# Later weight parts, earlier last stores and a moved row transpose in an RWKV and mixture-of-depths kernel

## The chip, the cores and the metric

The kernel runs on one core of one Trainium2 chip. The metric is the device time of one execution in microseconds (us); lower is better. A core has engines that each work through their own list of instructions in order: PE (matrix products and transposes), DVE (vector), ACT (scalar), POOL and SP, which here only issues transfers between the chip's memory (DRAM) and the on-chip buffers. Engines wait for each other through semaphores. Transfers are carried out by 16 DMA engines, which work beside all others.

## The reference

Two steps follow each other. The first is a linear attention over 768 time steps for 4 batches and 8 heads of 48 columns, with a state that decays:

```python
for t in range(S):
    kt, vt, rt = (k[:, :, t], v[:, :, t], r[:, :, t])
    cur = np.einsum('bhd,bhe->bhde', u[None] * kt, vt)
    y[:, :, t] = np.einsum('bhd,bhde->bhe', rt, state + cur)
    state = w[None, :, :, None] * state + np.einsum('bhd,bhe->bhde', kt, vt)
```

The second takes y, as rows of 384 columns, and lets the 128 rows with the highest score of each batch (of 768) pass through a two-layer network with 1024 hidden columns:

```python
scores = np.einsum('bsd,d->bs', x, w_gate)
out = x.copy()
for b in range(B):
    top_idx = np.argpartition(-scores[b], capacity)[:capacity]
    xe = x[b, top_idx]
    h = np.maximum(xe @ w1, 0.0)
    ye = h @ w2
    g = 1.0 / (1.0 + np.exp(-scores[b, top_idx]))
    out[b, top_idx] = x[b, top_idx] + g[:, None] * ye
```

All numbers are in 32-bit floating point.

## The kernel before

The time steps are cut into blocks of 128. There are 6 blocks in a batch and 24 in all (`NC` = 6, `NU` = 24). The main loop has one iteration per block. The order of all instructions on every engine is the order in which the program writes them down; no scheduler moves them.

**One iteration.** In iteration i PE finishes y of block i-1: first the products with the state (`from_state`, "y L287" from z and rh), then the score products of block i ("rp L259"), then the products with the values (`from_values`, "y L287" from vin and at). It then transposes k and r of block i+1 (`turn`, "L240", to the banks pt and st or ea), and makes the sums for the next state. These last exist in two forms: `state_product` (L269, 32 small matmuls in the profile, before the value products), used when `late` is true, and `state_products` (L282, 16 wider ones, after the turns) otherwise. `late` is true when work of the network is waiting in `queue` as the iteration begins. POOL writes half of the at-tile of the block (`diagonals`, L234), DVE writes the masked scores over it (`masked`, L302), and ACT copies y out (`leave_y`, the x-tile). At the end of an iteration POOL prepares k and r of block i+2 (L209, L213, L215). If `queue` is empty, PE ends the iteration with three products that nobody reads (`unread`, L264), in a bank that the next scores will use; they wait until DVE has read the bank's last contents.

**Choosing rows.** Scores are compared while the blocks come in. When a batch is complete, at iteration e+3 with e its last block (8, 14 and 20 for the first three batches), its rows are ranked (`rank`, `one_hot`), PE picks the indices (`pick`, L405), and POOL gathers the chosen rows from DRAM (`fetch`, an indirect transfer to xr, L417). For the first batch the pick stands at the end of iteration 8; for the others in the middle of theirs, behind up to two pieces of the network of the batch before. The gather reads what the stores of y have written, so it waits for the stores of its own batch. The program tells the dependency tracker that stores of other batches touch other rows. One iteration after the gather, at the place "chosen" at the end of the iteration, PE transposes the rows (`chosen`, L434, to bank pt), ACT copies them (xt), and `enqueue` puts 16 pieces into `queue`: eight times `hidden` (128 hidden columns, L467) and eight times `expert` (one product with 128 rows of the second matrix, L477). From then on every iteration takes its share of pieces, three in each of four iterations and two in each of the next two.

**The transfers.** All loads and stores of the loop are issued by SP, in the order in which they are written. At the head of iteration i these are k and r of block i+4 (L85, L86), v of block i+3 (two transfers, L92), some parts of the network's weights (L199 for the first matrix, L201 for the second), and the store of y of block i-2 (`store_y`, L335). SP runs through this list on its own; it only waits for buffers and for the x-tile that it stores. Inputs have six buffers, x has four.

**The weights.** Both matrices stay on the chip. They arrive in 20 parts: twelve of 128 rows and 256 columns of the first (128 KB each), ordered by groups of 256 columns and within a group by three blocks of rows, and eight of 128 rows of the second (192 KB each). `WEIGHTS` says how many parts iteration i issues. `hidden` with index f needs the three parts of its group (parts 0 to 2 for f = 0 and 1, 3 to 5 for f = 2 and 3, 6 to 8, 9 to 11), and `expert` with index f needs part 12+f. The tracker follows each part on its own: a product waits for the parts that it reads.

Of the kernel before, what the change touches and what calls it, by code (L numbers as in the profile page):

```python
# [17 lines left out]
def kernel(  # L18
# [16 lines left out]
    NC = S // T  # L35
# [42 lines left out]
    def load_kr(n):  # L78
        b, c = divmod(n, NC)
        rows = slice(c * T, (c + 1) * T)  # L80
        if n == 0:
            KIN[n] = kws[NKW - 1][:, :, :D]
        else:
            KIN[n] = work.tile([128, H, D], F32, name="kin", bufs=NIN)
        nc.sync.dma_start(out=KIN[n], in_=k[b, :, rows, :].rearrange("h t d -> t h d"))  # L85
        nc.sync.dma_start(out=rpads[n % NIN][:, :, :D], in_=r[b, :, rows, :].rearrange("h t d -> t h d"))  # L86

    def load_v(n):
        b, c = divmod(n, NC)
        for j in range(2):  # L90
            rows = slice(c * T + j * C, c * T + (j + 1) * C)
            nc.sync.dma_start(out=vins[n % NV][half(j), :, j, :], in_=v[b, :, rows, :].rearrange("h t d -> t h d"))  # L92
# [95 lines left out]
    for hp in range(NP):  # L188
        nc.scalar.activation(tr[:, hp, :C], up[:, hp, :C], AF.Copy, scale=winv[:, 0, hp : hp + 1])

    WEIGHTS = {i: 1 for i in range(3, 9)} | {9: 3, 10: 3, 11: 3, 12: 3, 13: 2}
    parts = [(q, kd) for q in range(4) for kd in range(KD)] + list(range(FB))

    def weights(n):
        for _ in range(n):
            j = parts.pop(0)
            if isinstance(j, tuple):
                f = slice(j[0] * F // 4, (j[0] + 1) * F // 4)
                nc.sync.dma_start(out=w1[:, j[1], f], in_=moe_w1[j[1] * 128 : (j[1] + 1) * 128, f])  # L199
            else:  # L200
                nc.sync.dma_start(out=w2[:, j, :], in_=moe_w2[j * 128 : (j + 1) * 128, :])  # L201
# [9 lines left out]
    def bonus(n):  # L211
        rk = work.tile([128, H, D], F32, name="rk")
        nc.gpsimd.tensor_mul(rk, rpads[n % NIN][:, :, :D], KIN[n])  # L213
        RKU[n] = work.tile([128, H, D], F32, name="rku")
        nc.gpsimd.tensor_mul(RKU[n], rk, ub)  # L215
# [75 lines left out]
    def from_state(n, hp, i, q):  # L291
        c = q ^ i
        z = Z1[n] if c else Z0.get(n)
        if z is not None:
            y_product(n, c, hp, i, RH[n][head(i), hp, half(c)], z[head(i), hp, :])
# [26 lines left out]
    def side(n, i):  # L322
        return YP[n][i][:, : NP * D].rearrange("t (p d) -> t p d", p=NP)
# [9 lines left out]
    def store_y(n):  # L333
        b, c = divmod(n, NC)
        st = nc.sync.dma_start(out=out[b, c * T : (c + 1) * T, :], in_=X[n])  # L335
        for (bb, _), others in moves.items():
            if bb != b:
                for o in others:
                    tc.declare_no_dep(st.ins, o.ins, reason="rows of another batch")
        stores.setdefault(b, []).append(st)  # L340
# [198 lines left out]
    def at(m, place, f, *a):  # L539
        fill.setdefault((m, place), []).append((f, a))  # L540

    def run(m, place):
        for f, a in fill.get((m, place), []):
            f(*a)
# [4 lines left out]
    for b in range(B - 1):  # L549
        e = b * NC + NC - 1  # L550
        at(e + 3, "start", rank, b)
        for z in range(NST):
            at(e + 3, "start", one_hot, b, z)
            at(e + 3, "pick" if b else "chosen", pick, b, z, "pt")
            at(e + 3, "fetch", fetch, b, z)
            at(e + 4, "chosen", chosen, b, z, "pt")
            at(e + 5, "middle", gate_sum, b, z)
            at(e + 6, "gate", gate, b, z)
            at(e + 4, "chosen", enqueue, b, z)

    def share(i):
        n = sum(f is not leave for f, _ in queue)
# [15 lines left out]
    def first():  # L578
        RP[0] = psum.tile([128, 2, 512], F32, name="rp")
        for hp in range(NP):  # L580
            for j in range(2):
                for c in range(2):
                    score_product(0, hp, j, c)
        turned(1, turn(rpads[1], "ea"))
        ST[0] = psum.tile([128, 512], F32, name="st")
        state_products(0)
        Z1[0] = work.tile([128, NP, D], F32, name="z1")
        nc.vector.tensor_copy(Z1[0], sums(0, 0))
        diagonals(0)
        masked(0)  # L590
        G[0] = work.tile([128, NP, D], F32, name="g")
        nc.vector.tensor_add(G[0], sums(0, 1), Z1[0])
        turned_k(1, turn(kws[1], "pt"))
        bonus_sum(1)
        diagonals(1)
        nc.vector.tensor_mul(wc, up[:, :, C], up[:, :, C])  # L596
        nc.vector.tensor_scalar(tri, jp, 0.0, None, op0=OP.is_lt)
        nc.scalar.copy(wg, spread(1, "eb"))
        scaled(2)
        bonus(2)  # L600

    for i in range(NU + 1):
        if i + 4 < NU:
            load_kr(i + 4)
        if i + 3 < NU:
            load_v(i + 3)
        weights(WEIGHTS.get(i, 0))
        if i > 1:
            store_y(i - 2)
        late = bool(queue)  # L610
        if not i:
            first()
            continue
        if i:
            if i < NU:
                t = psum.tile([128, 2, 512], F32, name="y")
                YP[i - 1] = [t[:, 0, :], t[:, 1, :]]
            else:
                YP[i - 1] = [psum.tile([128, 512], F32, name=name) for name in ("pt", "st")]
            for hp in range(NP):  # L620
                for j in range(2):
                    for q in (1, 0):
                        from_state(i - 1, hp, j, q)
            for j in range(1 if i < NU else 2):
                nc.scalar.copy(tiny[:, 1 : 1 + NP], side(i - 1, j)[C : C + 1, :, 0])  # L625
        if i < NU:
            if i not in RP:
                RP[i] = psum.tile([128, 2, 512], F32, name="rp")
            for hp in range(NP):
                for j in range(2):  # L630
                    for c in range(2):
                        score_product(i, hp, j, c)
            if late:
                for hp in range(NP):
                    for c in range(2):
                        for j in range(2):
                            state_product(i, hp, j, c)
        else:
            against_earlier(i - 2)
            score_row(i - 2, "y")  # L640
            against_own(i - 2)
            pieces(1)
        if i:
            for hp in range(NP):
                for c in range(2):
                    for j in range(2):
                        from_values(i - 1, hp, j, c)
        if i and i < NU:
            diagonal(i)
            if i > 3:  # L650
                diagonals(i)
            decays(i - 1)
        if i and i < NU:
            leave_y(i - 1)
            run(i, "gate")
        if i < NU:
            masked(i)
        run(i, "start")
        if late and i < NU:
            states(i)  # L660
        if i + 1 < NU:
            if i:
                turned_k(i + 1, turn(kws[(i + 1) % NKW], "pt"))
            turned(i + 1, turn(rpads[(i + 1) % NIN], "st" if late else "ea"))
        run(i, "turned")
        old = len(ready)
        leaving()
        if i < NU and not late:
            if i:
                ST[i] = psum.tile([128, 512], F32, name="st")  # L670
            state_products(i)
            states(i)
        m = share(i)
        if i < NU and m and (i, "pick") in fill:
            pieces(min(m, 2))
            m -= min(m, 2)
        run(i, "pick")
        if i + 1 < NU:
            bonus_sum(i + 1)
            if i < 3:  # L680
                diagonals(i + 1)
        if i and i < NU:
            gate_score(i - 1)
        run(i, "middle")
        if i < NU:
            pieces(m)
        if 2 <= i < NU:
            against_earlier(i - 2)
            score_row(i - 2, None if late or i != NC + 2 else "ea")
            against_own(i - 2)  # L690
        run(i, "last")
        if i + 1 < NU and not queue:
            RP[i + 1] = psum.tile([128, 2, 512], F32, name="rp")
            unread(RP[i + 1][:, 0, 384:], 3)
        run(i, "chosen")
        if i + 2 < NU:
            scaled(i + 2)
            bonus(i + 2)
        if i == 2:
            clear_v(5)  # L700
        if i == 4:
            numbers()
        send(old)
        run(i, "fetch")

    b, n = B - 1, NU - 1
# [65 lines left out]
```

## Time and profile before

| | us |
|---|---|
| median of three runs | 173.16 |
| the three runs | 173.14, 173.16, 176.85 |
| the profiled execution | 172.11 |
| span of its profile | 170.3 |

| engine | busy us | share of the span |
|---|---|---|
| PE (matmul) | 149.1 | 88% |
| PEld (weight load) | 127.1 | 75% |
| DVE | 110.4 | 65% |
| POOL | 103.9 | 61% |
| ACT | 97.6 | 57% |

The span covers the instructions; the execution's own time is 1.8 us longer. Transfers on SP's queue take 61.7% of the span of the 16 DMA engines, in 81612 packets, most of them under 512 bytes. The mean granted clock of PE is 0.97 of full speed.

In the slices of the profile page each digit is the busy share of a 40th of the span in tenths, and PEclk is the granted clock in tenths of full speed:

```profile
PE   5899999999996189996979967999998998997990
POOL 7999998997660792866562696986558331022022
PEclk9999999999999755999999999999999999999999
DMA  3999799866886997678898996898721112112000
```

A slice is 4.26 us. The profile's chain of waits follows the work that ended last back to what released it. "Issue" in it is time in which an engine waited for nothing that the profile shows. Timelines list instructions in order of time, merged where the same one repeats; the queue of SP lists the issue of each transfer, not its landing.

### The profile page before, as it was taken

The numbers are of one execution on the slowest core, as the hardware profiler recorded it, in microseconds if no ns is written. First come the engines' busy times: TensorE is split into PE (matmuls) and PEld (weight loads), VectorE is DVE, ScalarE is ACT, GpSimd is POOL, SyncE is SP. The second block draws the span as 40 slices with busy tenths as digits, with TensorE's granted clock in tenths as the row PEclk, the third lists the DMA queues.
The fourth block names the chain that finished last, engine by engine and source line by source line (L and its number), as shares of the span: only waits on it lengthen the run. The fifth ranks groups of instructions, "written<-read, shape, count | busy, mean of one in ns | idle before, by whom it ended". The sixth has DMA issues, their size and how long they took to land.

```text
span 170.3 us, 8282 instructions
## 1 busy us (share of the span) xinstructions
PE 149.1 (88%) x3475; PEld 127.1 (75%) x3475; DVE 110.4 (65%) x315; ACT 97.6 (57%) x346; POOL 103.9 (61%) x138
## 2 busy tenths in 40 slices
PE   5899999999996189996979967999998998997990
PEld 3677888988884179996848766998787797756990
DVE  5679988888980354768378479666975796733000
ACT  6656888886757026475637754875676867401200
POOL 7999998997660792866562696986558331022022
PEclk9999999999999755999999999999999999999999
DMA  3999799866886997678898996898721112112000
GB/s 67 179 187 168 143 175 188 198 144 119 191 199 154 183 214 188 144 178 230 183 233 209 206 198 125 182 220 169 157 98 50 50 52 94 48 18 80 0 20 26
DMA packets 82197, 24.13 MB, mean 142 GB/s; under 512 B 76126, under 2 KB 81792, under 8 KB 82160
## 3 DMA queue, kind: packets, MB, share of 16 engines
q1 hardware_dynamic: 81612, 22.03, 61.7%
q0 software_dynamic: 544, 1.57, 3.0%
q8 instruction: 27, 0.44, 1.1%
q14 instruction: 10, 0.08, 0.2%
q10 hardware_dynamic: 4, 0.00, 0.0%
HBM read 18.09 MB, written 5.51 MB: 139 GB/s over the span
## 4 chain that ended last, share of the span: by engine, by line
PE 64%; DMA 12%; issue 9%; DVE 5%; POOL 4%; ACT 3%; POOLq 1%; SPq 0%; ACTq 0%; DVEq 0%
PE y L287 13%; DMA xr<-out_dram,idx 7%; PE ea L467 7%; PE rp L259 6%; PE eb L467 6%; PE pt L240 5%; DMA w<-in_moe_w_dram 5%; PE eb L477 5%; PE st L282 3%; PE rp L269 3%; PE rp L264 3%; PE ea L240 3%; PE st L240 3%; PE ea L477 2%; ACT at L226 1%
## 5 line engine op out<-in xcount | busy, mean ns | idle before, releaser
L302 DVE COPY_PREDICATED at<-mask,rp 128x512 f32<-128x512 uint32 x24 | 17.8, 741 | 29.1 <-ACT at L226 10.1
L234 POOL TENSOR_TENSOR at<-dia,du 128x256 f32<-128x256 f32 x20 | 15.4, 769 | 23.3 <-DVE du L219 11.1
L226 ACT ACTIVATE at<-dia,du 128x64 f32<-128x64 f32 x96 | 25.5, 336 | 1.8 <-DVE du L219 1.8
L209 POOL TENSOR_TENSOR kw<-kin,wk 128x384 f32<-128x384 f32 x23 | 24.8, 1076 | 1.6 <-DMA kin<-in_k_dram 0.8
L215 POOL TENSOR_TENSOR rku<-rk,ub 128x384 f32<-128x384 f32 x24 | 24.5, 1020 | 1.9
L213 POOL TENSOR_TENSOR rk<-rpad,kin 128x384 f32<-128x384 f32 x23 | 23.4, 1016 | 1.5 <-DMA rpad<-in_r_dram 1.5
L318 ACT ACTIVATE z<-g,wc 128x48 f32<-128x48 f32 x80 | 19.9, 319 | 0.4 <-DVE wc L596 0.4
L259 PE MATMUL rp<-rh,kh 48*64 48x64 f32 x768 | 18.4, 229 | 1.0 <-DVE at L302 0.4
L417 POOL DMA_INDIRECT xr<-out_dram,idx x4 | 4.1, 1032 | 21.9 <-DVE part L485 10.1
L287 PE MATMUL y<-vin,at 64*64 64x48 f32 x736 | 16.8, 223 | 0.4 <-issue 0.4
L240 PE MATMUL pt<-ident,kw 128*128 128x128 f32 x96 | 16.6, 298 | 0.5 <-POOL rpad L139 0.4
L287 PEld LDWEIGHTS y<-z,rh 48*64 48x64 f32 x672 | 13.3, 138 | 4.8 <-issue 2.6
L259 PEld LDWEIGHTS rp<-rh,kh 48*64 48x64 f32 x768 | 15.4, 142 | 1.9 <-issue 1.0
L287 PE MATMUL y<-z,rh 48*64 48x48 f32 x672 | 16.3, 227 | 0.3 <-ACT x L331 0.3
L330 ACT COPY x<-y 64x192 f32<-64x192 f32 x46 | 14.4, 314 | 2.5 <-PE y L287 1.1
L344 DVE SCALAR_TENSOR_TENSOR scr<-x,wg 128x384 f32<-128x384 f32 x24 | 15.3, 637 | 0.7 <-ACT x L330 0.4
L287 PEld LDWEIGHTS y<-vin,at 64*64 64x64 f32 x736 | 14.3, 138 | 0.6 <-issue 0.6
L477 PE MATMUL ea<-w,ht 128*128 128x384 f32 x32 | 12.1, 497 | 2.4 <-DMA w<-in_moe_w_dram 2.4
L250 ACT COPY kh<-pt 128x512 f32<-128x512 f32 x23 | 13.6, 590 | 0.8 <-PE pt L240 0.8
L467 PE MATMUL eb<-xt,w 128*128 128x128 f32 x96 | 12.5, 278 | 1.4 <-issue 1.3
L625 ACT COPY tiny<-y 1x4 f32<-1x4 f32 x23 | 3.6, 157 | 17.2 <-PE y L287 17.2
L219 DVE TENSOR_REDUCE du<-rku 128x8 f32<-128x384 f32 x24 | 13.0, 543 | 0.0
(159 smaller groups left out, 306.6 us busy)
## 6 DMA issues: line engine op xcount, KB each, us to landing
rpad<-in_r_dram SPq DMA_DIRECT2D x24, 192.0 KB, 5.0
vin<-in_v_dram SPq DMA_DIRECT2D x48, 96.0 KB, 4.0
out_dram<-x SPq DMA_DIRECT2D x24, 192.0 KB, 3.5
kin<-in_k_dram SPq DMA_DIRECT2D x23, 192.0 KB, 4.3
w<-in_moe_w_dram SPq DMA_DIRECT2D x12, 128.0 KB, 3.4
w<-in_moe_w_dram SPq DMA_DIRECT2D x8, 192.0 KB, 4.1
kw<-in_k_dram SPq DMA_DIRECT2D x1, 192.0 KB
xr<-out_dram,idx POOLq DMA_INDIRECT x4, 3.7
```

What stands on the lines that cost most here:

```text
L209: (nc.gpsimd if n else nc.vector).tensor_mul(kws[n % NKW][:, :, :D], KIN[n], wk)
L213: nc.gpsimd.tensor_mul(rk, rpads[n % NIN][:, :, :D], KIN[n])
L215: nc.gpsimd.tensor_mul(RKU[n], rk, ub)
L226: nc.scalar.activation(AT[n][:, j, :], dia, AF.Copy, scale=du[:, j : j + 1])
L234: eng.tensor_mul(AT[n][:, h:, :], dia[:, None, :].to_broadcast([128, H - h, C]), du[:, h:, None].to_broadcast([128, H - h, C]))
L240: nc.tensor.transpose(t[:, hp, :], x[:, 2 * hp : 2 * hp + 2, :], ident)
L259: nc.tensor.matmul(out=RP[n][s, i, hp * C : (hp + 1) * C], lhsT=KH[n][head(i), hp, s], rhs=RH[n][head(i), hp, s], start=True, stop=True, s ...
L287: nc.tensor.matmul(out=YP[n][i][half(c ^ i), hp * D : (hp + 1) * D], lhsT=lhsT, rhs=rhs, start=(c, i) not in started, stop=True, skip_grou ...
L302: nc.vector.copy_predicated(at, causal, RP[n][:, :, : NP * C].rearrange("s i (p t) -> s i p t", p=NP))
L318: nc.scalar.activation(Z0[n + 1][:, hp, :], G[n][:, hp, :], AF.Copy, scale=wc[:, hp : hp + 1])
L467: nc.tensor.matmul(out=PE[b, z][:, f % 4, :], lhsT=w1[:, d, f * 128 : (f + 1) * 128], rhs=XT[b, z][d], start=(d == 0), stop=(d == KD - 1))
L477: nc.tensor.matmul(out=pe[:, : cols.stop - cols.start], lhsT=HT[b, z][:, f, :], rhs=w2[:, f, cols], start=(f == 0), stop=(f == FB - 1))
```

## The change

Three things are changed. The parts of the weights are issued in iterations 7 to 14 rather than 3 to 13. The stores of the last two blocks of a batch, which fall into iterations e+1 and e+2, are written ahead of the loads of their iteration instead of behind its weights. And for the first batch alone the transposes of the chosen rows, the copy of them and the filling of `queue` move from the end of iteration 9 to iteration 10, behind the turns of the next block, in bank eb instead of pt. Iteration 10 then begins with an empty queue, so `late` is false in it, and it uses the wider state products (L282).

```diff
-    WEIGHTS = {i: 1 for i in range(3, 9)} | {9: 3, 10: 3, 11: 3, 12: 3, 13: 2}
+    WEIGHTS = {7: 1, 8: 2, 9: 4, 10: 3, 11: 3, 12: 3, 13: 3, 14: 1}
...
-            at(e + 4, "chosen", chosen, b, z, "pt")
+            where = (e + 4, "chosen") if b else (e + 5, "turned")
+            at(*where, chosen, b, z, "pt" if b else "eb")
+            at(*where, enqueue, b, z)
             at(e + 5, "middle", gate_sum, b, z)
             at(e + 6, "gate", gate, b, z)
-            at(e + 4, "chosen", enqueue, b, z)
...
+    def next_store(i, ahead):
+        if i > 1 and ahead == ((i - 2) % NC >= NC - 2):
+            store_y(i - 2)
+
     for i in range(NU + 1):
+        next_store(i, True)
         if i + 4 < NU:
             load_kr(i + 4)
         if i + 3 < NU:
             load_v(i + 3)
         weights(WEIGHTS.get(i, 0))
-        if i > 1:
-            store_y(i - 2)
+        next_store(i, False)
```

The instructions of DVE, ACT and POOL stay the same in number. On POOL their order stays too; on DVE the r turn of iteration 10 now precedes the two state sums, and on ACT the copy of the chosen rows follows the k copy of iteration 10. SP issues the same transfers in another order. On PE only iterations 9 and 10 differ.

## What I expect, and how it is worked out

> **What bounds the kernel now.** I read the chain of waits in order of time first, then the timeline of POOL and of the SyncE queue (SP) around its two longest waits, then busy time by windows.
>
> The chain (start us, length us, what):
>
> ```profile
> 51.30 4.82 issue
> 56.31 4.61 DMA xr<-out_dram,idx
> 61.05 0.87 PE pt L434 x3
> ...
> 76.27 4.56 DMA w<-in_moe_w_dram
> 80.97 0.88 PE ea L477 x2
> ...
> 82.93 4.17 DMA w<-in_moe_w_dram
> 87.14 0.91 PE ea L477 x2
> ...
> 90.52 4.45 issue
> 95.18 4.11 DMA xr<-out_dram,idx
> 99.43 0.52 PE pt L434 x3
> ```
>
> The reader is to see four places where compute waits for memory: the gather of the chosen rows of batch 0 (at 56.31) and of batch 1 (at 95.18), each behind a wait of over 4 us, and between them two weight parts. Outside these the chain is PE work.
>
> POOL's and SP's timelines (start us, length us):
>
> ```profile
> 51.21 0.09 POOL L416 MEMSET spacer<- 1x1 f32 x1
> 56.31 1.18 POOL L417 DMA_INDIRECT xr<-out_dram,idx  x1 [5.01 <-issue]
> 57.52 0.62 POOL L234 TENSOR_TENSOR at<-dia,du 128x256 f32<-128x256 f32 x1
> ```
> ```profile
> 47.77 0.38 SPq L85 DMA_DIRECT2D kin<-in_k_dram  x1
> ...
> 51.00 1.60 SPq L199 DMA_DIRECT2D w<-in_moe_w_dram  x1
> 52.69 0.38 SPq L335 DMA_DIRECT2D out_dram<-x  x1
> ...
> 61.90 2.63 SPq L199 DMA_DIRECT2D w<-in_moe_w_dram  x3
> ```
>
> Counting stores from the first, 52.69 is y(5), the last rows of batch 0. Its x was copied in iteration 6, which ends at 39.6, 13 us earlier. So it is late because SP is: SP issues the transfers of its iteration 7 while PE is in iteration 9 (from 50.0). With the 3.5 us median landing of a store it lands near 56.2, where POOL's gather starts. The at-tile of iteration 9 (L234) stands behind the gather on POOL, the mask on DVE behind that, and PE idles from 53.72 to 58.96.
>
> Busy time by windows (us, PE, PEld, DVE, ACT, POOL, PEclk, DMA share, GB/s):
>
> ```profile
> 54.00:56.00 2.00, 0.00 (x0) 0.00 (x0) 0.00 (x0) 0.45 (x2) 0.00 (x0) 1.00 0.85 212
> ...
> 62.00:64.00 2.00, 2.00 (x80) 2.00 (x84) 0.08 (x2) 1.36 (x6) 1.93 (x3) 0.50 0.80 146
> ...
> 68.00:70.00 2.00, 2.00 (x32) 1.83 (x32) 1.97 (x7) 0.12 (x1) 1.25 (x2) 1.00 0.52 94
> ```
>
> After the idle stretch PE works at a granted clock of 0.50 until about 68. DMA stays at 0.8 to 0.9 while compute stands still. That is the decisive reading: from 20 to about 100 us SP is never held by compute (the buffers that it refills were released two or more iterations before). It runs at its own pace, and what counts is the order within it.
>
> **Pace of SP.** From the k load of i=3 (25.45) to that of i=9 (57.68) are six iterations with one weight part each: 5.37 us. From there to that of i=13 (86.11) are four with three parts: 7.11 us. So a part costs (7.11-5.37)/2 = 0.87 us; by the spacing of three in a burst (1.66 us from the first to the store behind them) 0.55. I take 0.8, nearer to the row that holds whole iterations. A store costs 0.5.
>
> **Part by part. First, stores and early parts.** Before y(5) no longer stand five parts (4.0) nor the k, r and v loads of i=7 (47.77 to 51.00: 3.2): issue at 52.69-7.2 = 45.5, landing near 49. The index is ready at 50.76 (reduction at 50.61, 0.15), so the gather starts when POOL reaches it, near 51.3: 5.0 us earlier. It lands about 55.5. POOL's at-tile ends at 53.3, the mask (0.73) at 54.0, and iteration 10 starts at 54.7 instead of 61.93. The moved stores hold SP for nothing: y(10) and y(11) are reached at about 77 and 85, their x is ready 3 or more us earlier. In batch 2, y(16) and y(17) may hold SP up to 0.5 us each (x done 110.10+0.32 and 114.74+0.32); behind them are loads for two iterations later: no cost. Y(4) moves before the loads of i=6, 0.5 us, repaid by three parts gone. Batch 3 has no loads left: nothing.
>
> **Chosen rows in iteration 10.** The three transposes (0.52 at full clock) and the xt copy (0.48) remain, only placed after the turns; the rows have landed by then. Iteration 10 is no longer "late": 32 state matmuls (L269, 0.45) become 16 wider ones (L282, 0.81): +0.36 on PE. The xt copy on ACT runs beside those. Bank eb is used instead of pt; its last reader is done an iteration before: nothing.
>
> **The price: every part is now due right after it is issued.** Parts are needed in order: hidden f=2 (iteration 10) needs parts 3-5, f=4,5 (iteration 11) 6-8, f=6,7 9-11, and expert f part 12+f. Their issue follows from what stands ahead in the queue, and landing from the row of the same burst:
> - Iteration 10: part 5 is third in the burst of i=9, three parts less ahead than the burst at 61.90: 61.90-2.4+1.3 = 60.8, landing +3.6 = 64.5. PE gets there at 54.7+0.61+0.48+0.47+0.59+0.44+0.52+0.81+1.34 = 60.0 (the chain's rows at full clock: from-state, scores, from-values, the two turns, chosen rows, state sums, f=0 and 1). It waits 4.5, and iteration 10 ends at 65.4 (before: 69.8).
> - Iteration 11: part 8: 69.69-1.6+0.7 = 68.8, landing +2.7 = 71.5. f=4,5 (1.34) and the score transpose (0.25) follow: end 73.0 (before 75.0).
> - Iteration 12: part 12 is third at i=11 rather than first: 76.27-1.6+1.3 = 76.0, +4.5 = 80.5; parts 10, 11 half a microsecond before it. f=6, f=7 and expert 0 then run in a row: end 81.9 (before 81.9). The lead is gone.
> - Iteration 13: part 15 is third at i=12, and the same parts plus y(10) stand ahead: landing 87.1+0.5: end 88.25 (before 88.1).
> - Iteration 14: part 17 now comes at i=13: 89.47-0.8+0.5 = 89.2, +3.8 = 93.0; PE is there at 91.7. Experts 4 and 5 precede the pick on PE, so the pick goes from 92.85 to 93.45, the index to 94.1. Y(11) landed at about 90, so the gather starts at 94.15 instead of 95.18.
> - Iteration 15: part 19, at i=14: 94.88-0.8+3.8 = 97.9. Experts and score transpose end at 98.6; the rows are there at 98.3. The transposes at L434 start at 98.6 instead of 99.43.
>
> From there PE is busy almost without a gap to 150 us and no part is outstanding: 0.83 us earlier is kept. Sum on the profiled execution: its 172.11 us (span 170.3) less 0.8 is 171.3. It lies 1.05 below the median of the three runs, so for the median: 173.16-0.8, rounded, 172.3.
>
> **A rule against the change.** In the trace 5.24 us of PE idle brought 0.50 from 57.68 on, 4 us into it, for 10.24 us; the 1.69 us idle before 99.43 brought nothing. The Trainium skill, "TensorE: Matmul & The Clock Gate" (Part 1), states that one idle window of about 3.4 us halves the clock until a like stretch of sustained work. By the rule and the first row the new 4.5 us wait in iteration 10 halves the clock again: iteration 11, 5.2 us at full clock, would end at about 74.6 rather than 73.0. By the second row (a wait cut to under 3 us) it would not. I take the halving, but count it at nothing: iteration 12 waits for part 11 until about 80 either way. Were the weights not the bound there, it would cost up to 1.6 us.
>
> **The rivals.**
> - *Weights in time (0.06 in full, 0.10 about halfway).* SP's gaps close when the early parts are gone, and part 5 lands by 60, 4.5 us before my reckoning. Then iteration 10 ends at 60.9 (8.9 gained), the part waits of 1.52 and 0.86 and the row wait of 1.69 go too: -13, 160. Halfway gives 167. For it: DMA share is only 0.65 from 38 to 42. Against: SP stood waiting for its queue there, not for compute, and loads alone fill some 4.5 us per iteration.
> - *Slower: part 19 holds iteration 15 (0.16).* The parts due at once come in larger bursts. The burst at 61.90 took 2.63 us, the one at 69.69 only 1.56: one stall of 1.07. If three of the bursts at i=9 to 13 stall so, part 19 lands 3.2 later, at 101.1, and holds the transposes and all behind: 173.16-0.8+3.2 = 175.5. It turns slower once part 19 lands after 98.8, 0.9 past my figure; over 2% needs 4.3 us.
> - *The store was not what held the gather (0.05).* Then the gather stays at 56.3; the L434 wait (0.44) moves, the weights bind as before: 173.
>
> **How the numbers follow.** My forecast gets 0.63. A measurement tells about 2% (3.5 us) from no change. Faster by that: the weights-in-time rival, full or halfway, 0.16. Slower: a third of the slow rival, 0.05. Within: 0.63+0.11+0.05 = 0.79. The range of 8 in 10 reaches from 169.0 (a quarter of the weights-in-time gain past my figure) to 175.0 (most of the slow rival); the forecast alone spans 170.8 to 173.8, a part's cost of 0.55 to 0.87 and landings of 2.7 to 4.5.
>
> **What would show it.** Y(5) issued near 45.5; the gather at about 51; no idle in iteration 9; a new PE wait at L467 for w in iteration 10, of 4 to 5 us, and smaller ones in 11 and 12; the gather of batch 1 near 94; L434 of iteration 15 less than 1.5 us earlier. I am wrong if SP reaches the burst of i=9 well before 59, or if PE finds its parts landed in iterations 10 to 15.

## The result, and the profile after

| | us |
|---|---|
| changed kernel, median of four runs | 170.18 |
| the four runs | 167.76, 168.30, 172.06, 174.69 |
| the kernel before beside it, median of four | 175.00 |
| ratio, with its 95% interval | 0.970 [0.964, 0.977] |
| the profiled execution; span of its profile | 167.76; 166.0 |

That ratio is the better end of what was seen, and its interval rests on two runs of each kernel (167.76 and 168.30 against 173.14 and 173.16). Two more comparisons, on two other chips, gave 0.9999 [0.9916, 1.0083] (medians 170.75 of 12 runs against 171.24 of 25) and medians of 170.29 (6 runs) against 172.94 (11), 0.985, without an interval. Ratios with an interval leave out executions that lay over 1.5% above the fastest of their kernel; medians are over all. Both kernels spread widely from run to run: the 25 runs of the kernel before on one chip lay between 167.72 and 176.21. So the change brought between nothing and 3%, by the medians of the two larger comparisons 0.5 to 2.7 us. The forecast was 172.3, 1.2% above the median of 170.18.

The 40 slices of the changed kernel's profile page (tenths busy; PEclk is the granted clock):

```profile
PE   5899999999998979687598999879999999997990
...
PEclk9999999999999999999999999999999999999997
DMA  3999789898979978887977997797511112111000
```

The hole of PE around slice 13 is gone, and so is the low clock behind it. In their place stands a row of smaller dents, slices 14 and 16 to 19 (counted from 0, 4.15 us each: 58 to 83 us), and two more at 25 and 26 (104 to 112 us). POOL's timeline and SP's (start us, length us, what; in brackets the idle time before and what ended it) show why the hole went:

```profile
48.30 0.09 POOL L416 MEMSET spacer<- 1x1 f32 x1
50.93 1.17 POOL L417 DMA_INDIRECT xr<-out_dram,idx  x1 [2.54 <-DVE idx L409]
52.14 0.62 POOL L234 TENSOR_TENSOR at<-dia,du 128x256 f32<-128x256 f32 x1
```
```profile
41.98 0.57 SPq L335 DMA_DIRECT2D out_dram<-x  x1
42.68 1.30 SPq L85 DMA_DIRECT2D kin<-in_k_dram  x1
...
46.74 0.61 SPq L199 DMA_DIRECT2D w<-in_moe_w_dram  x1
...
51.16 1.76 SPq L199 DMA_DIRECT2D w<-in_moe_w_dram  x2
...
57.02 2.53 SPq L199 DMA_DIRECT2D w<-in_moe_w_dram  x4
```

The store at 41.98 is y(5), 10.7 us earlier than before. The gather at L417 is now released by its index (DVE, L409) and starts at 50.93 instead of 56.31; the at-tile behind it on POOL is no longer late. The chain of waits (start us, length us, what) shows what took the place of the two gathers:

```profile
59.23 0.49 ACT kh L250
59.72 0.39 ACT xt L436
...
60.16 2.27 PE ea L467 x18
...
64.35 3.95 DMA w<-in_moe_w_dram
...
68.34 1.16 PE eb L467 x8
...
70.80 4.71 DMA w<-in_moe_w_dram
...
75.64 0.88 PE ea L477 x2
...
77.67 4.60 DMA w<-in_moe_w_dram
...
82.31 1.56 PE ea L477 x4
...
90.09 4.12 DMA w<-in_moe_w_dram
...
94.25 0.91 PE ea L477 x2
...
95.27 0.33 PE pt L434 x3
```

Four weight parts stand in the chain, 17 us of transfer, one in each of iterations 11, 12, 13 and 15. Counted by SP's issues they are parts 8, 12, 14 and 19; the prediction had named 15 in place of 14. PE's waits between 55 and 97 us (idle us, times, longest) say the same:

```profile
PE ea L477 <- DMA w<-in_moe_w_dram: 2.6, 2, 1.6
PE eb L467 <- DMA w<-in_moe_w_dram: 1.8, 3, 0.9
...
PE ea L467 <- ACT xt L436: 0.9, 1, 0.9
```

4.4 us of idle time is for parts, 3.6 and 5.6 in two more profiles of the changed kernel (of part 19 nothing here: it landed just as PE came to it; in the two other profiles PE waited 1.07 and 0.73 us for it). The third line is one that I had not expected: PE also waits for the copy of the chosen rows.

Where the gain went is seen best from iteration to iteration. The mark is ACT's small copy at the end of the products with the state (us from the span's start), in two profiles of the kernel before and three of the changed one:

| iteration | 10 | 11 | 12 | 13 | 14 | 15 | 16 | 23 |
|---|---|---|---|---|---|---|---|---|
| before | 63.1 | 70.6 | 75.8 | 82.7 | 88.9 | 94.0 | 100.7 | 139.6 |
| before, again | 62.5 | 70.3 | 75.5 | 80.9 | 86.0 | 91.6 | 98.9 | 137.4 |
| changed | 56.2 | 63.3 | 70.3 | 77.3 | 84.7 | 91.3 | 96.3 | 135.3 |
| changed, again | 56.4 | 63.4 | 73.0 | 81.2 | 86.3 | 92.0 | 98.3 | 137.0 |
| changed, third | 56.4 | 64.2 | 71.6 | 78.7 | 86.0 | 91.7 | 97.4 | 135.1 |

At iteration 11 the changed kernel leads by 6 to 7 us. At iteration 14 it lies between 4 us ahead and level, and at iterations 16 and 23 it leads by 2.5 and 2.7 in the means: most of the gain is given back between 11 and 14.

### The profile page after: what moved, and what is told of

The parts are those of the page before. It is cut to its first block, busy times and chain, and to the rows that moved or that the text cites. A ratio compares the mean times of both kernels' runs of the same rounds, so it can differ in the third digit from the quotient of the medians.

```text
span 166.0 us, 8250 instructions
## 1 busy us (share of the span) xinstructions
PE 148.0 (89%) x3459; PEld 124.7 (75%) x3459; DVE 109.8 (66%) x315; ACT 97.5 (59%) x346; POOL 103.2 (62%) x138
## 3 DMA queue, kind: packets, MB, share of 16 engines
q1 hardware_dynamic: 81612, 22.03, 62.4%
## 4 chain that ended last, share of the span: by engine, by line
PE 67%; DMA 12%; DVE 5%; issue 4%; ACT 4%; POOL 3%; SPq 2%; POOLq 1%; DVEq 0%; ACTq 0%
PE y L287 13%; DMA w<-in_moe_w_dram 10%; PE ea L467 6%; PE rp L259 6%; PE pt L240 6%; PE eb L467 6%; PE eb L477 5%; PE st L282 4%; PE ea L477 4%; PE rp L264 3%; PE ea L240 3%; PE rp L269 2%; PE st L240 2%; DMA xr<-out_dram,idx 2%; PE eb L369 2%
## 5 line engine op out<-in xcount | busy, mean ns | idle before, releaser
L240 PE MATMUL pt<-ident,kw 128*128 128x128 f32 x96 | 16.1, 292 | 0.5 <-POOL kw L140 0.5
L417 POOL DMA_INDIRECT xr<-out_dram,idx x4 | 4.1, 1029 | 19.2 <-DVE part L485 10.1
L344 DVE SCALAR_TENSOR_TENSOR scr<-x,wg 128x384 f32<-128x384 f32 x24 | 14.3, 598 | 0.7 <-ACT x L330 0.4
L467 PE MATMUL eb<-xt,w 128*128 128x128 f32 x96 | 13.0, 280 | 2.0 <-DMA w<-in_moe_w_dram 1.8
L467 PEld LDWEIGHTS eb<-xt,w 128*128 128x128 f32 x96 | 11.6, 192 | 2.8 <-DMA w<-in_moe_w_dram 2.4
```

The lines of the kernel that those rows point to most:

```text
L240: nc.tensor.transpose(t[:, hp, :], x[:, 2 * hp : 2 * hp + 2, :], ident)
L467: nc.tensor.matmul(out=PE[b, z][:, f % 4, :], lhsT=w1[:, d, f * 128 : (f + 1) * 128], rhs=XT[b, z][d], start=(d == 0), stop=(d == KD - 1))
```

## The experiments

The expectations name theories. A is the forecast's: a part costs SP about 0.8 us, the gain ends at the parts that are due right after their issue. Q: parts that are issued one at a time cost SP much more than 0.8, so the later weights alone bring y(5) forward. S: it is the place of the store in the queue that does. C: the main cost of the kernel before was the half clock behind the hole of PE.

### One part of the change at a time

Only the later weights:

```diff
-    WEIGHTS = {i: 1 for i in range(3, 9)} | {9: 3, 10: 3, 11: 3, 12: 3, 13: 2}
+    WEIGHTS = {7: 1, 8: 2, 9: 4, 10: 3, 11: 3, 12: 3, 13: 3, 14: 1}
```

> Of the change, only the later weight parts. Theory Q (the SP queue lost its time on weight parts issued singly: 1.2 to 1.4 us each against some 0.5 in a burst): the whole queue is earlier, so y(5) is issued near 47 even from its old place and lands before the index at 50.8; the gather starts near 51 and the time is within 1 us of the changed kernel, some 168 to 169 us. Theory A (my forecast's: 0.8 us a part wherever it stands): the parts bind in iterations 10 to 15 and the time is within 1 us of the kernel before. Theory S (the stores' place is what counts): y(5) is still behind loads and the part of i=7; less than half of the gain.

Only the two stores ahead of the loads:

```diff
     for i in range(NU + 1):
+        next_store(i, True)
         if i + 4 < NU:
...
-        if i > 1:
-            store_y(i - 2)
+        next_store(i, False)
```

> Of the change, only the two stores ahead of the loads. Y(5) should be issued near 47.8 and land near 51.3, so the gather starts near 51.5 in all theories, PE does not idle in iteration 9 and keeps its full clock. Theories Q and A: the queue behind is as slow as before, part 15 lands near 87.6, and only the wait of 1.7 us at the second gather is saved: 1 to 2 us faster than before. Theory S: the gather is the whole story, and the time is within 1 us of the changed kernel.

Only the chosen rows in iteration 10:

```diff
-            at(e + 4, "chosen", chosen, b, z, "pt")
+            where = (e + 4, "chosen") if b else (e + 5, "turned")
+            at(*where, chosen, b, z, "pt" if b else "eb")
+            at(*where, enqueue, b, z)
...
-            at(e + 4, "chosen", enqueue, b, z)
```

> Of the change, only the transposes of the first chosen rows in iteration 10. The gather stays at 56.3 and the idle stretch of PE with it. All theories: within 1 us of the kernel before (0.44 us of waiting for the rows removed, 0.36 us of wider state sums added).

And the first two together, without the third:

> The change without the moved transposes: later weights and earlier stores. PE then waits in iteration 9 for the rows, which land near 55.3, where it is ready at 55.5. Theories Q and A: within 0.7 us of the changed kernel. If the move carries the gain, 2 us or more slower than the changed kernel.

Measured, in one session on one chip (the kernel before: 172.02, median of 20; the changed kernel did not run in it):

| | median us (runs) | ratio | y(5) issued | gather | idle of PE in iteration 9 |
|---|---|---|---|---|---|
| weights | 172.94 (4) | 1.016 [1.005, 1.027] | 50.0 | 54.8 | 4.0 |
| stores | 171.46 (10) | 1.000 [0.993, 1.007] | 45.8 | 54.5 | none |
| moved rows | 173.80 (4) | 1.016 [1.000, 1.032] | 51.3 | 55.6 | 4.6 |
| weights and stores | 172.18 (10) | 1.005 [0.999, 1.012] | 44.3 | 53.7 | none |

No part by itself made the kernel faster. That two of them made it slower is not shown: their ratios compare all of four runs with the nine fastest of 20, and by the medians of all runs they are 1.005 and 1.010. Two expectations were missed: the moved rows lay 1.8 us above the kernel before by the medians (within 1 us expected), and the stores alone did not bring theory A's 1 to 2 us. POOL's and SP's timelines of the kernel with only the later weights:

```profile
54.75 1.18 POOL L417 DMA_INDIRECT xr<-out_dram,idx  x1 [6.38 <-DMA out_dram<-x]
```
```profile
49.29 0.61 SPq L199 DMA_DIRECT2D w<-in_moe_w_dram  x1
49.99 0.60 SPq L335 DMA_DIRECT2D out_dram<-x  x1
```

The gather is released by the landing of a store, which is what the forecast inferred and the trace of before had booked as "issue". A second profile of the kernel before names the store too:

```profile
55.84 1.17 POOL L417 DMA_INDIRECT xr<-out_dram,idx  x1 [7.33 <-DMA out_dram<-x]
```

Four parts fewer ahead of y(5) brought it forward by 0.5 to 2.7 us (it was issued at 50.5 to 52.7 in the four profiles that have the old queue), 0.1 to 0.7 a part. Theory Q falls: y(5) would have had to be near 47. POOL's timeline with only the stores ahead:

```profile
51.87 0.09 POOL L416 MEMSET spacer<- 1x1 f32 x1
54.49 1.18 POOL L417 DMA_INDIRECT xr<-out_dram,idx  x1 [2.53 <-DVE idx L409]
```

Here the index releases the gather, 2.53 us behind the spacer as in the changed kernel. (In this execution PE worked at half its pace until about 21 us, against about 10 in the kernel before: four transposes of k took 1.11 us at 17.0, there 0.66 at 14.5. So its compute times are not to be set beside those of the others; its gather is late with its index.) So the store's place is enough to open the gate and the weights are not, which is S. As the whole story S falls: its ratio is 1.000. The windows view of the same kernel (us; PE, PEld, DVE, ACT, POOL busy; granted clock, DMA share, GB/s) shows a part wait taking its place, with a half clock behind it:

```profile
76.00:78.00 2.00, 0.08 (x1) 0.11 (x2) 1.07 (x4) 0.53 (x1) 1.90 (x3) 1.00 0.64 192
...
80.00:82.00 2.00, 2.00 (x86) 2.00 (x82) 0.21 (x1) 1.98 (x9) 0.00 (x0) 0.50 0.92 179
```

PE stands from 75.9 to 77.9 for part 12. The kernel with weights and stores stops for 2.37 us among the value products of iteration 11, for nothing that the profile shows, and in iteration 13 for 1.74 us, for part 13.

### The half clock taken away, the late gather kept

To the kernel before, 22 products that nobody reads are added in the hole of iteration 9:

```diff
+                if i == 9:
+                    unread(psum.tile([128, 512], F32, name="pt")[:, :128], 22)
```

> The kernel before, with 22 more products that nobody reads in iteration 9, so that PE is not idle while it waits for the mask. The gather stays late. Theory C (the half clock after the idle stretch is the main cost of the late gather): iteration 10 runs at full clock, 2 to 3 us faster than before. Theories Q and A: the parts of the network's second matrix are not earlier, so PE waits longer for them in iterations 12 and 13, and less than 1 us is gained.

Measured: 172.41 (6 runs) against 171.24, ratio 1.018 [1.008, 1.028], by the medians of all runs 1.007. From its windows, POOL's timeline and its chain:

```profile
62.00:64.00 2.00, 2.00 (x115) 1.83 (x114) 0.00 (x0) 1.30 (x5) 1.04 (x2) 1.00 0.84 257
```
```profile
94.98 0.99 POOL L417 DMA_INDIRECT xr<-out_dram,idx  x1 [7.67 <-DMA rpad<-in_r_dram]
```
```profile
94.98 4.27 DMA xr<-out_dram,idx
...
99.39 0.52 PE pt L434 x3
```

The granted clock stayed at 1.00 until 105 us, and iteration 10 took 5.1 us (63.2 to 68.3) instead of the 7.5 and 7.8 of the kernel before. Iteration 11 began 2 us earlier, and the index of the second gather was there at 91.0. Yet that gather still started at 95.0 and L434 at 99.39, against 99.43 and 97.66 in the two profiles of the kernel before: none of the 2 us was kept. That y(11) held the gather, which this queue issued at 89.2, is argued: it is the last store that the gather reads, but the profile books the wait to a load of r that landed at the same moment. In iteration 9 the products overshot the hole: the rows had landed at 59.1, and L434 started at 61.96. The time lost against the kernel before comes later, in 2.05 us of idle PE before 103.5, which the profile books to ACT, and a half clock from 105.0 to 108.5. C falls: in this profile a gain of PE alone between iterations 10 and 15 is worth nothing while the queue stays as it is.

### The parts' due times

If the parts bind, issuing them ahead of the k, r and v loads of their iteration, which are needed three and four iterations later, should give time back, and later parts should cost. To the changed kernel:

```diff
         next_store(i, True)
+        weights(WEIGHTS.get(i, 0))
         if i + 4 < NU:
             load_kr(i + 4)
         if i + 3 < NU:
             load_v(i + 3)
-        weights(WEIGHTS.get(i, 0))
```

> The changed kernel, with each iteration's weight parts ahead of its k, r and v loads. Parts are issued some 3.5 us earlier; the loads, which are needed two iterations later, some 2 us later. Theory A (late parts are what is left): most of the 4.9 us of PE waiting for parts in iterations 11 to 13 goes, and the time falls by 2 to 4 us against the changed kernel. If SP's pace binds in every case, the waits move to the k and r loads and less than 1 us is gained.

Measured: 168.50 (12 runs) against 171.24 for the kernel before, ratio 0.981 [0.968, 0.994], an interval that rests on two of its runs (by the medians 0.984); the changed kernel in the same session 170.75. Its waits of PE:

```profile
PE eb L467 <- DMA w<-in_moe_w_dram: 3.7, 3, 2.3
PE ea L477 <- DMA w<-in_moe_w_dram: 3.5, 4, 1.2
```

In this execution (169.83) parts are still waited for, 7.2 us in these lines. They lead the transfers of their iteration, but the queue as a whole was later here: parts 5, 8 and 12 were issued at 58.1, 64.5 and 71.4, at most 2 us earlier than in the changed kernel, and part 19 at 91.5, no earlier. So the expected 3.5 us did not come, and this profile does not show where the gain of the median comes from. The next kernel has the same order, with parts an iteration earlier:

```diff
-    WEIGHTS = {7: 1, 8: 2, 9: 4, 10: 3, 11: 3, 12: 3, 13: 3, 14: 1}
+    WEIGHTS = {7: 3, 8: 4, 9: 3, 10: 3, 11: 3, 12: 3, 13: 1}
```

> Weights first as in the experiment before it (ratio 0.981 to the kernel before), and the parts themselves an iteration earlier: 3, 4, 3, 3, 3, 3, 1 in iterations 7 to 13, behind the early stores. The profile of weights first still showed PE waiting 7.3 us for parts from 60.7 to 90.4. If the parts' due times are what is left, most of that goes, and the time is 1 to 3 us below weights first, 165.5 to 167.5 us; if SP's pace as a whole binds, the waits move to the k and r loads and the time stays at 168 to 169.

Measured: 167.32 (163.44 to 171.02, 6 runs) against 172.94 (169.72 to 179.52, 11), with no interval, and the changed kernel in the same session 170.29. In its profile, the slowest of the six runs, v loads held PE for 3.1 us and parts for 1.5. The two ranges overlap, so the same kernel ran again on another chip:

> Parts earlier and first once more, for an interval against the kernel before: 167.3 us median in six runs against 172.9 so far. Between 0.96 and 0.98 if that holds.

Measured: 166.03 (161.74 to 169.83, 6 runs) against 173.46 (170.47 to 177.09, 17). Here the ranges do not touch; medians give 0.957, and 0.967 in the session before. It is the fastest version that ran. Its waits of PE from 55 to 95 us:

```profile
PE rp L269 <- DMA vin<-in_v_dram: 1.7, 3, 1.1
...
PE pt L434 <- DMA xr<-out_dram,idx: 1.1, 1, 1.1
...
PE ea L477 <- DMA w<-in_moe_w_dram: 0.3, 1, 0.3
```

Here the parts were issued 5 to 7 us earlier than in the changed kernel (part 5 at 52.6, part 19 at 85.5). Of the changed kernel's 4.4 us for parts 0.3 is left; v loads, which now stand behind the parts, cost 1.7. The marks of iterations 11 to 14 (62.4, 67.6, 72.9, 78.0) keep the lead through the stretch where the changed kernel loses it.

The opposite: all parts of the changed kernel one iteration later, in its own order of the queue.

```diff
-    WEIGHTS = {7: 1, 8: 2, 9: 4, 10: 3, 11: 3, 12: 3, 13: 3, 14: 1}
+    WEIGHTS = {8: 1, 9: 2, 10: 4, 11: 3, 12: 3, 13: 3, 14: 3, 15: 1}
```

> The changed kernel with every weight part one iteration later still (8 to 15), the suspected cost doubled. If the parts' due times bind from iteration 10 to 15, as my forecast had it, PE waits some 5 us for part 5 in iteration 10 and part 19 comes with the loads of i=15, some 5 us later: 174 to 177 us, 3% or more above the changed kernel. If the parts had slack and PE is the bound there, the time stays within 1 us of the changed kernel.

Measured: 175.60 (10 runs) against 173.46 for the kernel before, ratio 1.013 [1.004, 1.022]; the changed kernel did not run beside it. PE's timeline and the chain:

```profile
67.99 1.87 PE L467 MATMUL ea<-xt,w 128*128 128x128 f32 x6 [4.12 <-DMA w<-in_moe_w_dram]
```
```profile
99.40 3.95 DMA w<-in_moe_w_dram
...
103.40 0.91 PE ea L477 x2
...
104.42 0.33 PE pt L434 x3
```

Here is the wait that the forecast had put into the changed kernel's iteration 10, 4.12 us for the first of parts 3 to 5, and part 19 holds L434 of iteration 15 until 104.4. The slower rival's mechanism is real; the changed kernel lies one iteration short of it.

### Repeats

> The kernel before once more, for a second profile. In every theory y(5) is issued near 52 again, the gather starts 4 us or more after the index, and PE's clock is cut in iteration 9 or 10. The pace of SP is the open point: if it is fixed, the k load of i=14 is issued within 1 us of 91.9.

Measured: 169.56. The k load of iteration 14 went out at 90.3, against 91.9 in the first profile: the pace of SP is not fixed. The rest came as expected: y(5) at 52.3, the gather 5.5 us behind its index, the clock cut at 57.7.

> The changed kernel once more, with more rounds, since the runs of both kernels spread over 4%. If the first comparison (0.970) holds, 0.96 to 0.98; if it was the luck of four runs each, 0.98 to 1.00. The runs so far say that a run's time goes with its share of half clock, so the changed kernel should show fewer such stretches than the kernel before.

Measured: the ratio of 0.9999 given above. PE's timeline and windows of its profiled execution (168.91):

```profile
69.09 2.50 PE L467 MATMUL eb<-xt,w 128*128 128x128 f32 x10 [2.46 <-DMA w<-in_moe_w_dram]
```
```profile
68.00:70.00 2.00, 0.91 (x4) 0.91 (x5) 0.00 (x0) 0.00 (x0) 1.92 (x3) 0.68 0.71 180
70.00:72.00 2.00, 2.00 (x19) 1.67 (x20) 0.00 (x0) 0.15 (x1) 0.87 (x1) 0.50 1.03 192
```

Part 7 landed at 69.05, 2.1 us later than in the first profile; PE stood 2.46 us for it in one piece (there 0.51 for part 7 and 0.88 for part 8), and the clock was at 0.50 for 10.2 us. That is the second line of changed marks in the table, 2.6 us behind at iteration 12, 3.9 at 13, 0.7 at 15.

> The changed kernel a third time, beside the others on one chip, since the first comparison gave 0.970 and the second 1.000. My forecast's 0.8 us is 0.995. Between 0.98 and 1.00 the forecast's size stands; below 0.975 the first comparison was right.

Measured: 170.29 against 172.94, as above; its marks are the third changed line.

## Why the prediction was right or wrong

**The gate.** Right in cause: the gather waited for the store of y(5) (the kernel with only the weights and the second profile of the kernel before show it by name), and the store's place opens it (the kernel with only the stores). PE's idle stretch in iteration 9 went, and with it the half clock there. The gather was forecast at 51.3 and came at 50.9 to 51.9. PE was to start iteration 10 at 54.7 and did at 55.4; the mark in it is 56.2 to 56.4, against 63.1 and 62.5 before.

**Y(5) and the pace of SP.** Mis-sized. "Issue at 52.69-7.2 = 45.5" measured 42.0, 42.5 and 43.9 in the changed kernel. One part of that was in the profile: the loads and the part of i=7 that y(5) moves past take 4.92 us from 47.77 to 52.69, where the sum put 3.2+0.8, because that part's issue alone took 1.60. The rest is a deeper error: "it runs at its own pace" was read from one execution, and the pace varies. Times of the k loads on SP:

| k load of iteration | 7 | 9 | 13 |
|---|---|---|---|
| before | 47.8 | 57.7 | 86.1 |
| before, again | 46.5 | 57.1 | 82.1 |
| old queue (moved rows only) | 47.9 | 56.6 | 85.3 |
| old queue (unread products) | 46.0 | 55.7 | 83.0 |
| changed, three profiles | 42.7, 43.2, 44.6 | 53.5, 53.9, 54.9 | 79.2, 80.3, 80.5 |

One queue reaches iteration 13 up to 4 us apart, and my profile was the latest of four. The changed kernel is there 4.1 us earlier in the mean (84.1 less 80.0), with two parts fewer and one store more issued by then; by the forecast's own costs that is 1.1. At iteration 9 the count of parts still holds: three parts fewer, 2.7 us in the means, 2.4 by the forecast. The surplus arises between 9 and 13. So the parts were issued 1 to 5 us before the forecast's times. In the three profiles part 5 landed at 61.0 to 62.8 (forecast 64.5), part 8 at 68.3 to 69.5 (71.5), part 12 at 75.4 to 76.8 (80.5), part 19 at 94.2 to 95.9 (97.9), and the gather of batch 1 started at 89.6 to 91.2 (94.15). What sets the pace, and why it was faster by about 3 us than the count of parts says, the runs do not show.

**Rows moved to iteration 10.** "The xt copy on ACT runs beside those" failed. ACT works in order and reaches xt at 59.72, behind its at, z, x and kh copies; PE waits 0.92 us for it and starts on the hidden products at 60.16. The wait is the same 0.9 us in all three profiles. How much of it costs time differs: without it PE would have come to f=2 near 60.16+1.34-0.92 = 60.6, and part 5 landed at 61.0, 61.8 and 62.8, so some to all of it is covered. Alone the move had no gain to show (1.016 [1.000, 1.032]).

**The price.** Right in cause, late by one iteration in place. "It waits 4.5, and iteration 10 ends at 65.4" did not occur: with part 5 there 2 to 3.5 us sooner and PE there later, iteration 10 waits for a part in one profile of three, 0.2 us, and the first long wait is in iteration 11, for parts 7 and 8. From there parts hold PE in every iteration to 13 in two profiles, and part 19 holds iteration 15, as forecast; in the profile with the half clock only iterations 11 and 15 wait. Part 17, which was to hold iteration 14, held nothing. The forecast had named two signs of being wrong, and both came in part: SP reached the burst of i=9 at 57.0, 57.6 and 58.8, and in iterations 10 and 14 PE found its parts landed. Later parts bring the 4 us wait back, earlier ones take the waits away and are faster than both kernels: so it is the parts' due times that took the gain back.

**What is kept.** "The transposes at L434 start at 98.6 instead of 99.43", held by part 19. PE waited for part 19 in two of the three profiles and found it just landed in the third, but L434 started at 95.3, 97.1 and 96.3 in the three profiles, against 99.4 and 97.7 before. About 2.3 us kept in the mean, instead of 0.8. This is the pace term again, through the landing of part 19. On the median of the runs shown that makes 173.16-2.3 = 170.9; that session measured 170.18. That the forecast of 172.3 lies so near is in part luck: a queue up to 5 us faster than reckoned, the wait for xt (0.9) and the half clock, both put at nothing, pull in opposite directions.

**The half clock.** The rule quoted before, and counted at nothing, deserved a little. In one of three profiles of the changed kernel the clock was cut in this stretch, by a wait of 2.46 us, less than the 3.4 us of that rule; that profile's L434 is the latest of the three, by 0.8 to 1.8 us. The second half of the reasoning, that parts bind anyway and would swallow it, holds for most of the 3.9 us lost at iteration 13: at iteration 15 0.7 is left, at 16 2.0.

**The rivals.** Weights in time: partly, in that the bursts came earlier than reckoned, yet four parts were waited for; the version with earlier parts is that rival made true, and with 166 to 167 it gave what "halfway" had put down (167). Slower, with all three edits in, was only the kernel whose parts come later still. That the store was not the gate is excluded.

**Left open.** The size: 0.970, 0.985 and 1.000 on three chips are not reconciled beyond the spread of single runs. The first is past the 2% to which the forecast gave 0.16, the others are within what it called most likely. Weights with the moved rows, and stores with the moved rows, were not tried, so how much of the changed kernel's lead over the one with weights and stores only (1.005 in another session) belongs to the move is not shown.

## What to carry to other kernels

A store that a gather reads belongs ahead of the prefetches of its queue; where it stands, not how much is in the queue, opened the gate here. A load that is moved later gets a due time, and that is to be worked out for each one from the place in the queue. Those due soonest go ahead of prefetches that have iterations to spare, and early enough: the order alone left 7.2 us of waiting, order and an earlier iteration together 0.3 and 1.5 in two profiles. Take the pace of a queue from several executions before counting tenths of a microsecond with it, and judge an effect of 1% in a kernel that spreads by 4% from a dozen runs at least (12 runs against 25 gave an interval of 0.8% to either side).

## What the runs showed of the hardware

- A short stop is enough to halve the clock: 2.02 us of PE idle in the kernel with only the stores, 2.46 in the changed one. A stop of 2.28 us in the version with weights first left it at 1.00:

```profile
67.88 1.37 PE L467 MATMUL eb<-xt,w 128*128 128x128 f32 x9 [2.28 <-DMA w<-in_moe_w_dram]
```
```profile
68.00:70.00 2.00, 2.00 (x51) 1.81 (x55) 0.19 (x1) 0.27 (x1) 0.00 (x0) 1.00 1.04 208
```

  (PE's timeline and windows of that version.) So the length of the stop alone does not decide, and its place counts: in these profiles the clock changes on a grid. In the records of the granted clock the cuts of one execution lie whole multiples of 3.41 us apart (57.74 and 98.70 in the second profile of the kernel before, 12 of them; 67.47, 84.53 and 105.02 with later parts, 5 and 6), and inside the kernel half clock lasted 3.41, 6.83 or 10.24 us, one to three of them. The 3.41 us before the cut hold all 2.02 us of the first stop and 2.1 of the second; that of weights first falls on an edge of its grid, at 66.31 (counted back from its one cut, at 168.71), which leaves 0.7 and 1.6 us. PE was busy for 1.39 and 1.31 us of the 3.41 before these two cuts, and for 1.85 where none followed. Over all profiles cuts followed stretches with up to 1.84 us of busy PE, and stretches with about 1.5 us and more also passed without one, so the exact limit is not shown.
- The spread between runs goes in part with the half clock. From the mean clock c of a run, the time at half clock is 2(1-c) of its time. In the mean that is 14.6 us a run in the kernel before (25 runs), 9.2 in the changed one (12), 5.1 with weights first (12) and 4 to 5 with earlier parts (two sessions of 6). Some of it falls at the very end, where PE is done (2.1 us in the first profile of the changed kernel). The correlation with a run's time is 0.48, 0.59 and 0.24 in the first three, and 0.74 to 0.84 in three other sessions of the kernel before (11 to 20 runs).
